# A new issue order for the five queues of a fused attention and state-space kernel

## The chip, the cores and the metric

The kernel runs on one core of a Trainium2 chip. The core has five instruction queues that matter here: TensorE (PE, matmuls, with its weight loads counted apart as PEld), VectorE (DVE), ScalarE (ACT), SyncE (SP) and GpSimd (POOL). Each executes its own list of instructions in the order in which the list is written, and the queues wait for one another by semaphores. SP, ACT and POOL also issue DMA transfers, which then run beside the engines. The metric is the device time of one execution in microseconds. Three executions are shown, and their median is the kernel's time.

## The reference

Two independent parts are computed from bfloat16 inputs, and their outputs are put side by side into one array of 1 x 2048 x 1280.

```python
def _A_ref(x, wqkv, wo):              # S = 2048, D = 640, 32 heads of 20
    qkv = (x @ wqkv).reshape(B, S, 3, H, Dh).transpose(2, 0, 3, 1, 4)
    q, k, v = qkv[0], qkv[1], qkv[2]
    off = arange(8) * 2               # each position sees itself and 7 before it, in steps of 2
    logits = einsum("bhsd,bhswd->bhsw", q, kg) * Dh ** -0.5
    attn = softmax(where(mask, logits, -1e9))
    o = einsum("bhsw,bhswd->bhsd", attn, vg)
    return o.transpose(0, 2, 1, 3).reshape(B, S, D) @ wo

def _B_ref(u, A_re, A_im, B_re, B_im, C_re, C_im, log_dt, Dskip):   # L = 2048, D = 640, N = 192
    dt = exp(log_dt)[:, None]
    P = exp((dt * (A_re + 1j * A_im))[:, :, None] * arange(L))
    K = einsum("dn,dnl,dn->dl", C, P, dt * B).real
    y = irfft(rfft(u padded to 2L) * rfft(K padded to 2L))[:L]
    return y + u * Dskip
```

## The kernel before

The state-space part works on five chunks of 128 channels (NCH = 5). It starts with a preparation (`partB_prep`). `load` (L127 to L132) brings the parameters in, each in four quarters u = 0 to 3 of 32 partitions. Of `B_A_re`, ACT's queue loads the quarters 0 and 2, and SP's the quarters 1 and 3 (L131). `decays` (L168) turns `B_A_re` times dt into columns: PE multiplies a quarter with a diagonal matrix DG (L156 on DVE; L163 and L166 on PE, into `ps_tr`), and ACT copies each quarter from `ps_tr` into `alpha`, a part of the tile LPB (L173). `fill` (L175) is DVE's work on `B_A_im`: dt·A_im/2π is reduced and split into three bfloat16 pieces, hi (L186), mid (L188) and lo (L189), once for the first chunk (128x192: `hi_188`, `mid_189`, `lo_190`) and once for the four others (128x768: `hi_367`, `mid_368`, `lo_369`). Transfers of SP and POOL (L194) move the pieces into the tile LPA; one transfer carries the pieces of both planes of a quarter. `weights` (L221 to L228, the tiles p10, p11, p20, p21 and CN) and `coefficients` (L237, the tile cT) prepare B times C. SP also loads U (four transfers of 640 KB, L914), the constants T2 (1 MB, L907), EA and BD, and Dskip (Dn).

For each chunk, `exps_chunk` fills the table R with ACT's Exp (L256) from LPB's `alpha`, which every instruction reads over all four quarters. `phase_table` fills the tables TA and TX with ACT's Sin (L311) from PE's products of LPA (`ps_ph`, L303 and L307). Exp and Sin use different tables of ACT, so each change costs an ACT_TABLE_LOAD. DVE multiplies R with TA and TX into PG, Q and X (L332) and PG with k's power into Y (L366); PE sums X·Y over the states into the convolution kernel (L380, L385). Then come the Fourier stages: PE and ACT (L399 to L408), DVE's products (L432), the inverse on PE and ACT (L445, L446), a transfer of half a spectrum by SP (L415, P2 and Zdram), and u·Dskip (UD, DVE's L460, moved to `UDdram` by POOL, L461).

The attention part starts in the last chunk: projections of k (L553), q (L571) and v (L584), a halo of k (`k_halo`, L562), products and logits (L604, L615), softmax, the weighted sum of v (DVE's L690 and PE's L697 into `ps_o`) and the output projection (L732 on). The inverse transform of the state-space part ends between them (L787).

What sets the order is a table. The program is written as one long function (`body`), which records instructions in a natural order. At its end `pin` (L866) goes through the five strings of `ORDER` (L808), one for PE, DVE, ACT, SP and POOL in turn. A string lists runs "start+count" in hexadecimal, counted in the engine's own instructions as recorded, and `pin` chains each instruction to the one before it in that list. This is a dependence without a semaphore: it only fixes the queue's order. Waits for data between the engines come from the tiles as before. A second table, `PLACES`, sets which bank of PSUM a product uses.

Of the kernel before, what the change touches and what calls it, by code (L numbers as in the profile page):

```python
# [744 lines left out]
class Inverse:  # L745
# [63 lines left out]
    '3+3 0+3 6+6 54+c c+8 1c+8 38+4 40+4 78+c 2c+8 60+c 14+8 24+8 6c+c 84+c 48+4 50+4 34+4 3c+4 90+c 44+4 4c+4 a8+c 9c+c b4+8 c4+8 bc+8 cc+8 e0+4 e8+4 '  # L809
    '35c+c 374+c d4+8 380+c dc+4 e4+4 9a4+c fc+80 ec+4 f4+4 f0+4 f8+4 2fc+10 17c+80 32c+10 31c+10 9b0+c 30c+10 1fc+c0 344+8 354+8 2bc+40 34c+8 33c+8 368+c '  # L810
    '394+8 3a4+8 3b4+4 3bc+4 3d4+80 3c8+4 3d0+4 3b8+4 3c0+4 38c+8 39c+8 3c4+4 3cc+4 454+40 3ac+8 4e4+10 494+40 504+10 9bc+c 4f4+10 4d4+10 534+80 524+8 '
    '51c+8 514+8 5b4+80 52c+8 654+10 634+20 664+10 704+80 694+8 6a4+8 9c8+c 68c+8 674+8 784+40 6b4+c 6c4+4 67c+8 7c4+40 684+8 6c0+4 6c8+8 6d4+4 69c+8 6ac+8 '
    '6d0+4 6d8+c 6ec+8 6e4+8 6f4+10 814+80 914+10 804+10 924+10 894+40 934+20 8d4+40 954+20 9f4+80 974+10 a74+40 984+8 ab4+40 99c+8 98c+8 af4+80 ec8+c '
    '994+8 9d8+4 9e0+4 b74+40 9d4+4 9dc+4 bb4+40 9e8+4 9f0+4 9e4+4 9ec+4 c24+10 c04+10 ed4+c bf4+10 c54+8 c64+8 c14+10 c9c+40 c34+10 c5c+8 c6c+8 c44+8 '
    'cdc+40 c80+4 c88+4 c4c+8 ee0+c c7c+4 c84+4 c8c+4 c94+4 c74+8 d1c+40 c90+4 c98+4 d6c+40 e2c+20 d5c+10 dac+40 e4c+20 dec+40 e8c+10 e7c+10 e6c+10 f34+40 '
    'ea4+10 f74+40 ebc+c e9c+8 eb4+8 fb4+40 eec+8 efc+8 ff4+40 ef4+8 f04+14 f1c+4 1034+40 f24+4 f2c+4 f18+4 f20+4 1074+40 f28+4 f30+4 10d4+10 10b4+20 '
    '1388+c 10e4+10 111c+8 112c+8 1394+c 10fc+8 10f4+8 114c+4 1154+4 115c+40 1104+10 13a0+c 1150+4 1158+4 1114+8 1124+8 1134+8 119c+40 113c+4 1144+4 1140+4 '
    '1148+4 11dc+50 12fc+10 12ec+10 134c+10 130c+20 122c+40 132c+20 126c+80 1364+10 135c+8 137c+c 13f4+40 1374+8 1434+40 13ac+8 13bc+8 1474+40 13d4+4 '
    '13dc+4 13b4+8 13c4+8 14b4+40 13d8+4 13e0+4 14f4+40 13cc+8 1588+8 1598+8 13e8+4 13f0+4 13e4+4 13ec+4 1590+8 15a0+8 1534+40 15a8+8 1574+14 15b4+4 15bc+4 '
    '15d0+4a 15b0+4 15b8+4 16a4+10 161a+40 169a+a 16b4+10 17ce+19 15c0+4 15c8+4 16d4+10 16c4+10 165a+40 1704+a 15c4+4 15cc+4 170e+80 16fc+8 16e4+8 178e+40 '  # L820
    '17e7+a 16ec+8 18b1+a 16f4+8 17f1+80 18bb+a 18d9+4a 18c5+a 1871+40 18cf+a 1923+40 19f9+10 19cb+a 1963+68 19e9+10 1a27+10 1a09+a 1a37+10 1a6b+10 19d5+14 '
    '1a5b+10 1a7b+10 1a13+14 1a8b+10 1af7+a 1a9b+10 1a47+14 1b01+a 1ab3+8 1acf+28 1aab+8 1abb+14 1b0b+a 1b1d+a 1b51+a 1b37+a 1b27+10 1b6b+a 1b41+10 1b5b+10 '
    '1b15+8 1b85+14 1b75+10 1bc1+50 1c4d+28 1c39+14 1c11+28 1c75+14 1b99+28 1cb5+3c 1cb1+4 1c89+28 1cf1+14 1d2d+3c 1da1+4 1d05+28 1dc5+8 1d69+28 1dcd+28 '
    '1d91+10 1da5+20 1e15+4 1df5+10 1e1d+4 1e05+10 1e21+10 1e51+8 1e31+10 1e19+4 1e7d+2 1e41+10 1e59+4 1ea1+c 1e9f+2 1ecd+2 1ee3+2 1e5d+10 1ef5+4 1ecf+4 '
    '1e6d+10 1e7f+20 1ead+20 1ed3+10 1ee5+10 1ef9+8 1f11+4 1f4f+a 1f2a+5 1f01+10 1f15+15 1f2f+20 1f5e+5 1f59+5 1f6f+10 1f63+4 1f7f+30 1fb9+4 1f67+8 1faf+a '
    '1fbd+4 2001+5 1fc1+20 2015+8 2006+5 1fe1+10 2061+5 1ff1+10 200b+a 201d+4 2066+5 2021+40 2075+c 206b+a 2081+20 20c1+a 20a1+10 20d5+4 20b1+10 20dd+20 '
    '20d9+4 20fd+8 2109+10 2105+4 2119+10 20cb+a 2129+1a 2173+a 2143+30 217d+20 21c7+a 21a7+20 21a2+5 219d+5 21db+a 21d6+5 21d1+5',
    '0+1 3+1 5+1 4+1 8+1 a+1 2+1 9+1 7+1 6+1 b+1 10+1 1f+1 21+1 e+1 1e+1 20+1 11+1 22+1 12+2 16+1 d+1 23+1 17+1 14+1 24+1 18+1 15+1 27+1 19+2 c+1 1b+2 28+1 '
    '2f+2 34+1 33+1 1d+1 35+1 31+1 36+1 25+1 32+1 29+1 37+2 26+1 39+1 2a+2 3b+1 f+1 2c+2 3a+1 2e+1 3c+1 3e+3 3d+1 41+1 44+1 48+1 42+1 45+1 43+1 47+1 46+1 '
    '4b+1 49+2 4c+2 50+1 5e+1 4f+1 4e+1 51+2 57+1 62+1 54+1 53+1 58+1 55+2 5b+1 5a+1 59+1 5d+1 5c+1 70+1 60+1 5f+1 61+1 63+1 65+3 64+1 6a+1 1+1 76+1 68+1 '  # L830
    '6d+1 84+1 6e+1 69+1 6b+1 88+1 74+1 6c+1 9d+1 6f+1 73+1 75+1 ad+1 79+1 71+2 77+2 7a+1 7d+1 b1+1 7b+2 81+1 7e+3 86+1 82+2 87+1 85+1 89+1 8b+2 8a+1 8d+2 '
    '96+1 95+1 90+1 8f+1 9b+1 91+1 93+1 92+1 9c+1 97+1 94+1 9a+1 99+1 98+1 9e+4 a4+2 a2+1 a6+1 a3+1 a7+1 aa+1 a8+1 ab+2 c6+1 ae+1 a9+1 af+2 b2+1 b4+2 b3+1 '
# [345 lines left out]
```

## Time and profile before

| | us |
|---|---|
| median of three runs | 390.82 |
| lowest, highest run | 389.01, 391.63 |
| the profiled execution's span | 389.9 |
| PE busy (8677 matmuls) | 338.0 |
| DVE busy | 356.1 |
| ACT busy | 311.8 |
| PE, longest waits for its own instructions on the chain | 2.16, 2.06, 2.00, 1.95 |

The profile is one execution. A line of a timeline has the start, the length, the engine, the line of the kernel, the operation, the tile written and the tile read, the number of instructions it puts together, and in brackets the idle time before it and what ended that. "SPq" and "ACTq" are the issuing of transfers by these queues. A line of a stretch has its start and end, its length, the busy time of PE, PEld, DVE, ACT and POOL (with the count of instructions), the granted PE clock as a share of full speed, the DMA engines' busy share, and GB/s. A line of the waits has who waited for whom: in total, how often, and the longest.

### The profile page before, as it was taken

What the parts mean: (1) busy time and instruction counts of PE and PEld (TensorE: products, weight loads), DVE (VectorE), ACT (ScalarE), POOL (GpSimd) and SP (SyncE); (2) the same over time, 40 slices, a digit from 0 to 9 for tenths busy, and PEclk for the clock granted to TensorE, in tenths of its full rate; (3) what the DMA queues carried; (4) which work ended last, traced back from release to release, by engine and by line L of the source; (5) the groups of instructions that cost most, each with busy time, mean ns of one, the idle gap of its engine ahead of it and who ended that gap; (6) DMA issues with size and microseconds to landing.
All of it is one profiled execution on the core that took longest, in us unless ns stands there. A gap on an engine that the chain in (4) does not pass through costs nothing.

```text
span 389.9 us, 18862 instructions
## 1 busy us (share of the span) xinstructions
PE 338.0 (87%) x8677; PEld 250.9 (64%) x8677; DVE 356.1 (91%) x353; ACT 311.8 (80%) x524; POOL 49.9 (13%) x102
## 2 busy tenths in 40 slices
PE   1286989788898899988888999999999997789993
PEld 0275878677787778877777576556656775344561
DVE  8989899997999999999999998999988996897971
ACT  3999999799999999999998766455987746576761
POOL 8545001021000000100000100000030100011220
PEclk9998899699999999999999999999999999788998
DMA  6499304035021410151049662110773589399254
GB/s 161 109 192 208 121 13 163 6 103 121 29 84 34 109 32 31 57 131 40 2 118 152 144 133 71 34 30 2 166 248 100 163 192 204 70 254 282 81 141 110
DMA packets 39471, 43.30 MB, mean 111 GB/s; under 512 B 24768, under 2 KB 33952, under 8 KB 38752
## 3 DMA queue, kind: packets, MB, share of 16 engines
q1 hardware_dynamic: 34384, 29.34, 32.4%
q0 software_dynamic: 4112, 12.22, 11.5%
q8 instruction: 68, 1.11, 1.3%
q10 hardware_dynamic: 896, 0.54, 0.5%
q14 instruction: 11, 0.09, 0.1%
HBM read 19.63 MB, written 14.16 MB: 87 GB/s over the span
## 4 chain that ended last, share of the span: by engine, by line
PE 44%; ACT 25%; DVE 18%; issue 6%; DMA 4%; SPq 2%; POOL 0%; ACTq 0%; DVEq 0%; POOLq 0%
ACT R L256 7%; PE ps_k L553 6%; PE ps_q L571 6%; PE ps_v L584 6%; DVE Y L366 5%; ACT A L408 4%; DVE X L332 4%; PE ps_o L697 3%; ACT A L403 3%; PE ps_k L380 3%; PE ps_k L385 3%; PE ps_op L732 3%; PE ps_l L615 2%; PE ps_ia L445 2%; PE ps_f L399 2%
## 5 line engine op out<-in xcount | busy, mean ns | idle before, releaser
L366 DVE TENSOR_TENSOR Y<-PG 128x3072 bf16<-128x3072 bf16 x60 | 102.9, 1750 | 3.0 <-PE ps_k L385 2.8
L256 ACT ACTIVATE R<-LPB 128x192 bf16<-128x192 f32 (+1 forms) x169 | 57.7, 420 | 0.1
L380 PE MATMUL ps_k<-Y,X 128*32 128x64 bf16 x2176 | 46.9, 240 | 7.0 <-issue 2.7
L385 PE MATMUL ps_k<-Y,X 64*32 64x64 bf16 x2176 | 45.5, 234 | 0.7 <-issue 0.6
L380 PEld LDWEIGHTS <-X 128*32 128x32 bf16 x2176 | 34.8, 117 | 15.4 <-issue 6.8
L408 ACT CAST A<-ps_f 128x1024 bf16<-128x1024 f32 x40 | 40.4, 1038 | 3.5 <-PE ps_f L407 3.4
L385 PEld LDWEIGHTS <-X 64*32 64x32 bf16 x2176 | 32.8, 113 | 8.8 <-issue 1.1
L332 DVE TENSOR_TENSOR X<-R,TX 128x1536 bf16<-128x1536 bf16 x40 | 37.3, 950 | 0.3 <-PE ps_k L385 0.3
L311 ACT ACTIVATE TX<-ps_ph 128x768 bf16<-128x768 int16 x40 | 32.2, 838 | 3.7 <-PE ps_ph L307 3.7
L690 DVE TENSOR_TENSOR prod<-v,atp 128x1536 bf16<-128x1536 bf16 (+3 forms) x32 | 31.6, 1022 | 3.7 <-PE ps_o L697 3.7
L303 PE MATMUL ps_ph<-LPB,LPA 128*64 128x256 bf16 x288 | 29.3, 308 | 4.0 <-ACT A L408 1.3
L311 ACT ACTIVATE TA<-ps_ph 128x768 bf16<-128x768 int16 x30 | 24.3, 843 | 1.8 <-PE ps_ph L307 1.7
L407 PE MATMUL ps_f<-A,T 128*128 128x128 bf16 x320 | 22.3, 217 | 3.3 <-ACT A L408 1.3
L604 DVE TENSOR_TENSOR prod<-qT,kT 128x1024 bf16<-128x1024 bf16 (+1 forms) x16 | 22.9, 1486 | 1.2 <-ACT qT L572 0.8
L584 PE MATMUL ps_v<-xT,wv 128*32 128x512 bf16 x400 | 23.2, 379 | 0.0
L553 PE MATMUL ps_k<-xT,wkq 128*128 128x512 bf16 x100 | 23.1, 380 | 0.0
L407 PEld LDWEIGHTS <-T 128*128 128x128 bf16 x320 | 19.1, 96 | 6.1 <-issue 3.3
L571 PE MATMUL ps_q<-xT,wkq 128*128 128x512 bf16 x100 | 22.6, 379 | 0.0
L446 ACT CAST Z<-ps_ia 128x1024 bf16<-128x1024 f32 x20 | 19.6, 1014 | 3.4 <-PE ps_ia L445 2.2
L401 ACT ACTIVATE A<-ps_f,sign 128x1024 bf16<-128x1024 f32 x20 | 21.5, 1149 | 0.2 <-PE ps_f L399 0.2
L332 DVE TENSOR_TENSOR PG<-R,TA 128x768 bf16<-128x768 bf16 (+1 forms) x30 | 19.8, 685 | 1.8 <-ACT TA L311 1.3
L399 PE MATMUL ps_f<-BD,U 128*64 128x128 bf16 x320 | 21.0, 285 | 0.1
(157 smaller groups left out, 696.1 us busy)
## 6 DMA issues: line engine op xcount, KB each, us to landing
P<-A SPq DMA_DIRECT2D x16, 256.0 KB, 3.1
Zdram<-Z SPq DMA_DIRECT2D x16, 256.0 KB, 3.7
Z<-Zdram SPq DMA_DIRECT2D x8, 512.0 KB, 7.0
U<-in_B_u_dram SPq DMA_DIRECT2D x4, 640.0 KB, 9.5
UDdram<-UD POOLq DMA_DIRECT2D x10, 256.0 KB, 2.7
Z<-UDdram POOLq DMA_DIRECT2D x4, 640.0 KB, 6.7
out_dram<-ysb SPq DMA_DIRECT2D x32, 80.0 KB, 3.9
out_dram<-ob POOLq DMA_DIRECT2D x8, 160.0 KB, 3.4
```

The source lines that it names most:

```text
L256: exp = lambda o, i, m: nc.scalar.activation(out=o, in_=i, func=ACT.Exp, scale=m)
L311: last = nc.scalar.activation(out=dst, in_=words.rearrange("p b (q e f) -> p b q (e f)", e=8, f=4), func=ACT.Sin, scale=PI_LO / 32768.0)
L332: TT = lambda o, a, b, op: V.tensor_tensor(out=o, in0=a, in1=b, op=op)
L366: nc.vector.tensor_tensor(out=Y[:].rearrange("p q (b a) f -> p q b a f", a=8), in0=fa, in1=gb, op=A.mult)
L380: MM(ps[32 * g:32 * g + 32, t], lhsT=X[:, q, x, :, f], rhs=Ys[k][:, q, :, f], start=(t == 0 and n == 0), stop=False, tile_position=(0, 32 ...
L385: MM(ps[32 * g:32 * g + 32, t], lhsT=X[hb, q, x, :, f], rhs=Ys[k][hb, q, :, f], start=False, stop=(n == len(sets) - 1), tile_position=(64 ...
L407: last = MM(ps[:, kk], lhsT=C["T2"][:, 8 * b + kk, :], rhs=A1[:, :, 8 * b + kk, :], start=(kk % 4 == 0), stop=True, skip_group_check=True)
L408: nc.scalar.copy(out=A1[:, :, 8 * b:8 * b + 8, :], in_=ps[:].rearrange("p k (j g) -> p j k g", g=4))
L553: MM(ps[:, i], lhsT=self.wk[:, kt, 128 * ct:128 * ct + 128], rhs=self.x4[:, kt, 2 * i:2 * i + 2, 256 * hf:256 * hf + 256], start=(kt == 0) ...
L571: MM(ps[:, i], lhsT=self.wq[:, kt, 128 * ct:128 * ct + 128], rhs=self.x4[:, kt, 2 * i:2 * i + 2, 256 * hf:256 * hf + 256], start=(kt == 0) ...
L584: MM(ps[32 * sc:32 * sc + 32, i], lhsT=self.wv[:, kt, d + i::DH], rhs=self.xT[:, kt, 512 * sc:512 * sc + 512], start=(kt == 0), stop=(kt = ...
L690: nc.vector.tensor_tensor(out=p2.rearrange("p (d i) -> p d i", i=ni), in0=self.v2[:, 4 * j0:4 * j0 + 4 * nj, off:off + ni], in1=at[:, w, i ...
```

## The change

Only the five strings of `ORDER` differ. `PLACES`, the tiles, the instructions and their operands are the same; the file grows by nine lines, so that every line below the table has a number higher by nine (L914 becomes L923). The beginning of SP's string, before and after:

```diff
-    '2+1 1+1 0+1 3+1 19+1 c+1 7+1 4+1 14+1 6+1 d+1 a+1 9+1 8+1 17+1 1a+1 b+1 e+2 5+1 11+1 10+1 15+1 13+1 12+1 1e+2 18+1 20+1 23+2 1b+2 22+1 21+1 1d+1 16+1 '
...
+    '0+3 a+1 6+1 d+1 9+1 c+1 7+1 5+1 b+1 8+1 24+1 1a+1 17+1 f+1 16+1 1e+1 13+1 1c+1 11+2 15+1 e+1 10+1 19+1 3+1 21+2 4+1 23+1 18+1 1f+1 1b+1 14+1 1d+1 20+1 '
...
```

SP's queue at its start. The two loads of `B_A_re` (the quarters 1 and 3) stand in its rows 3 and 7 before. The first eight transfers before:

```order
L123 DMA ldt_105<-in_B_log_dt_dram 32x20 x2
L1140 DMA ident_58<-ident_c 128x128
L132 DMA B_A_re_112<-in_B_A_re_dram 32x5x192
L909 DMA Dn_223<-in_B_Dskip_dram 32x160
L132 DMA B_C_re_138<-in_B_C_re_dram 32x5x192
L140 DMA mix_124<-c_mix 128x288
L132 DMA B_A_re_112<-in_B_A_re_dram 32x5x192
L905 DMA BD_75<-c_BD 128x512
```

The same queue now, its rows 16 to 27:

```order
L194 DMA LPA_101<-lo_190 32x2x192
L194 DMA LPA_101<-mid_368 32x2x576
L194 DMA LPA_101<-hi_188 32x2x192
L194 DMA LPA_101<-mid_189 32x2x192
L915 DMA EA_77<-c_EA 128x256
L194 DMA LPA_101<-hi_188 32x2x192
L194 DMA LPA_101<-lo_190 32x2x192
L918 DMA Dn_223<-in_B_Dskip_dram 32x160
L132 DMA B_A_re_112<-in_B_A_re_dram 32x5x192
L194 DMA LPA_101<-mid_368 32x2x576
L194 DMA LPA_101<-lo_369 32x2x576
L132 DMA B_A_re_112<-in_B_A_re_dram 32x5x192
```

The two loads now stand in rows 24 and 27. Ahead of these rows, from row 3, come the other parameters and constants, then U (row 11), Dn, mid_189 (row 13), T2 (row 14) and U again (row 15).

DVE's queue at the end of the preparation, with the second plane's mid_368 and lo_369. Before:

```order
L187 TENSOR_TENSOR m1_388<-tg32_381,hi_367 128x768
L188 CAST mid_368<-m1_388 128x768
L221 TENSOR_TENSOR p11_554<-B_B_re_128,B_C_im_143 128x768
L189 TENSOR_TENSOR lo_369<-m1_388,mid_368 128x768
L223 TENSOR_TENSOR p11_554<-p11_554,p21_555 128x768
L226 TENSOR_SCALAR CN_125<-p11_554,dts_154 128x192 x4
L332 TENSOR_TENSOR PG_577<-R_231,TA_279 128x1536
```

And now:

```order
L189 TENSOR_TENSOR lo_369<-m1_388,mid_368 128x768
L221 TENSOR_TENSOR p10_545<-B_B_re_128,B_C_re_138 128x768
L221 TENSOR_TENSOR p10_421<-B_B_re_128,B_C_re_138 128x192
L223 TENSOR_TENSOR p10_545<-p10_545,p20_546 128x768
L223 TENSOR_TENSOR p10_421<-p10_421,p20_422 128x192
L221 TENSOR_TENSOR p11_427<-B_B_re_128,B_C_im_143 128x192
L222 TENSOR_TENSOR p21_555<-B_B_im_133,B_C_re_138 128x768
L223 TENSOR_TENSOR p11_554<-p11_554,p21_555 128x768
L226 TENSOR_SCALAR CN_125<-p11_554,dts_154 128x192 x4
L223 TENSOR_TENSOR p11_427<-p11_427,p21_428 128x192
L226 TENSOR_SCALAR CN_125<-p10_421,dts_154 128x192
L226 TENSOR_SCALAR CN_125<-p11_427,dts_154 128x192
```

The pieces are finished earlier in DVE's list, and the weights, those of the first chunk included, stand behind them. PG (L332) follows in both.

ACT's queue around its first table of exponentials, R. Before, its rows 6 to 15:

```order
L132 DMA B_A_re_112<-in_B_A_re_dram 32x5x192
L173 COPY LPB_102<-ps_tr_168 128x48
L173 COPY LPB_102<-ps_tr_173 128x48
L173 COPY LPB_102<-ps_tr_178 128x48
L173 COPY LPB_102<-ps_tr_183 128x48
L256 ACTIVATE R_231<-LPB_102 128x48x4 x42
L237 CAST cT_167<-ps_tr_433 128x4x48
L256 ACTIVATE R_231<-LPB_102 128x48x4 x3
L311 ACT_TABLE_LOAD
L311 ACTIVATE TA_279<-ps_ph_280 128x2x384
```

And now, the rows 8 to 19:

```order
L173 COPY LPB_102<-ps_tr_178 128x48
L173 COPY LPB_102<-ps_tr_183 128x48
L256 ACTIVATE R_231<-LPB_102 128x48x4 x23
L237 CAST cT_167<-ps_tr_433 128x4x48
L256 ACTIVATE R_231<-LPB_102 128x48x4 x6
L237 CAST cT_167<-ps_tr_447 128x4x48
L256 ACTIVATE R_231<-LPB_102 128x48x4 x2
L237 CAST cT_167<-ps_tr_475 128x4x48
L256 ACTIVATE R_231<-LPB_102 128x48x4 x7
L237 CAST cT_167<-ps_tr_461 128x4x48
L256 ACTIVATE R_231<-LPB_102 128x48x4 x7
L173 COPY LPB_102<-ps_tr_489 128x4x48
```

The copies of cT, which use DVE's CN by way of PE, now lie among R's exponentials. Then follow the table load and the first TX, ahead of the two TA. Over the rest of the program runs of instructions change places in the same manner on all five engines. Among them, the last transposes of x on SP and `k_halo` on PE stand later, DVE's UD steps (L460) too, and the outputs on SP are spread differently.

115 rows, old and new, of the table ORDER are left out of this document.

## The prediction

> **What bounds the kernel now.** I read the page's busy times first, then the chain of waits, then a table of stretches. The busy lines say that no engine is full from end to end; the chain's shares say that TensorE, ScalarE (ACT) and VectorE (DVE) each carry a part of the end; only the stretches say where.
>
> ```profile
> span 389.9 us, 18862 instructions
> PE 338.0 (87%) x8677; PEld 250.9 (64%) x8677; DVE 356.1 (91%) x353; ACT 311.8 (80%) x524; POOL 49.9 (13%) x102
> PE 44%; ACT 25%; DVE 18%; issue 6%; DMA 4%; SPq 2%; POOL 0%; ACTq 0%; DVEq 0%; POOLq 0%
> 0.00:8.56 8.56, 1.29 (x12) 0.90 (x12) 6.81 (x21) 2.29 (x7) 7.40 (x19) 1.00 0.61 151
> 8.56:33.02 24.46, 15.10 (x220) 12.98 (x221) 23.17 (x48) 22.75 (x68) 12.87 (x24) 1.00 0.93 164
> 33.02:128.75 95.73, 83.04 (x2803) 71.23 (x2801) 89.93 (x80) 93.56 (x169) 11.14 (x22) 0.93 0.29 82
> 128.75:213.76 85.01, 75.94 (x2392) 65.72 (x2386) 84.68 (x72) 82.50 (x130) 2.81 (x6) 1.00 0.31 75
> 213.76:329.00 115.24, 114.18 (x2220) 74.33 (x2217) 108.57 (x89) 77.28 (x90) 7.49 (x19) 1.00 0.51 122
> ```
>
> In the last five lines stand the stretch, its length, then the busy time of PE, its weight load, DVE, ACT and POOL. From 8.56 to 128.75 ACT is the full engine (22.75 of 24.46, then 93.56 of 95.73). DVE takes over until 213.76 (84.68 of 85.01), and PE until 329 (114.18 of 115.24). So a late start of ACT is carried from one full engine to the next, and only their small idle remains can absorb it. What releases ACT at 8.56 is the place to look at, in ACT's and SP's timelines:
>
> ```profile
> 8.33 0.20 ACT L173 COPY LPB<-ps_tr 128x48 f32<-128x48 f32 x1 [0.91 <-PE ps_tr L166]
> 8.56 3.65 ACT L256 ACTIVATE R<-LPB 128x192 bf16<-128x192 f32 x14
> 2.13 0.72 SPq L132 DMA_DIRECT2D B_A_re<-in_B_A_re_dram  x1
> 4.94 0.57 SPq L132 DMA_DIRECT2D B_A_re<-in_B_A_re_dram  x1
> DMA to landing us min/median/max: 2.6/2.8/3.0
> ```
>
> The exponentials R (L256) need the decay table LPB. It is written by four copies (L173), one for each quarter of B_A_re, behind PE transposes (L163, L166). Two quarters are loaded by SP, at 2.13 and 4.94; a transfer lands 2.6 to 3.0 us behind its issue. So the last lands by 7.9, and R begins at 8.56, some 0.7 later.
>
> **The change, part by part.** No instruction is added, removed or resized, so the busy times stay; only places in five queues differ.
>
> *SP's two loads.* They go from rows 3 and 7 of SP's queue to rows 24 and 27, behind seven transfers that carry DVE's pieces (mid, lo, hi) and behind U twice, T2 and EA. In the profile such a transfer holds its queue while its data are missing, and SP also stands after large ones:
>
> ```profile
> SPq L194 <- DVE m L187: 1.9, 2, 1.6
> 17.18 0.59 SPq L194 DMA_DIRECT2D LPA<-mid  x1
> 17.82 2.11 SPq L914 DMA_DIRECT2D U<-in_B_u_dram  x2
> 19.97 3.32 SPq L909 DMA_DIRECT2D Dn<-in_B_Dskip_dram  x1
> 24.04 4.97 SPq L914 DMA_DIRECT2D U<-in_B_u_dram  x2
> 29.05 4.48 SPq L194 DMA_DIRECT2D LPA<-hi  x1
> ```
>
> The first line is SP waiting at L194 for DVE, in total 1.9 us in 2 waits: the queue does not pass over a transfer that isn't ready. The last load now stands behind lo_369, the last piece that DVE makes. When is lo_369 made? DVE works almost without a gap through this preparation in the profile:
>
> ```profile
> 4.09:27.97 23.88, 23.50 (x63) 1.00 0.85 167
> 24.18 0.95 DVE L221 TENSOR_TENSOR p<-B_B_re,B_C_im 128x768 f32<-128x768 bf16 x1
> 25.05 0.95 DVE L189 TENSOR_TENSOR lo<-m,mid 128x768 bf16<-128x768 f32 x1
> 25.92 0.95 DVE L223 TENSOR_TENSOR p<-p,p 128x768 f32<-128x768 f32 x1
> 26.90 1.07 DVE L226 TENSOR_SCALAR CN<-p,dts 128x192 bf16<-128x192 f32 x4
> L221 DVE TENSOR_TENSOR p<-B_B_re,B_C_re 128x192 f32<-128x192 bf16 x1 | 0.3, 350 | 0.0
> ```
>
> (The first line is the stretch 4.09 to 27.97 with DVE's busy time alone: 0.4 idle.) The same steps in another order, with no more idle, still end at 27.97, ahead of L332. Behind lo_369 the new order has four steps of 128x768, four of 128x192 and six CN (L226). A 128x768 step takes 0.87 from its start to the next (24.18 to 25.05); a 128x192 one, 0.35 less the same overlap of 0.08, 0.27; a CN 1.07/4, with its share of the step, 0.25 as an estimate. That is 3.48 + 1.08 + 1.5 = 6.06, so lo_369 is ready at 27.97 − 6.06 = 21.9, and mid_368, one step ahead, at 21.0. mid_368's first transfer is SP's row 17 and the last load row 27: eleven issues. An issue is 0.58 to 0.61, with 0.04 between two (17.18 to 17.82 is 0.64). Ten steps put the last issue's start at 21.0 + 6.4 = 27.4. lo_369 is long ready then, so mid_368 sets the pace. The load lands 2.8 later, at 30.2, and R begins 0.7 behind that: 30.9, if SP never stands.
>
> Upper end: SP stands behind U and T2 as long as it stood in the rows above, 3.32 at Dn less a plain 0.6, and 4.48 less 0.6: 2.7 + 3.9 = 6.6, so R at 37.7. I take R at 32.2, nearer the lower end: one U and T2 are in flight when the loads' turn comes (the other U is issued ahead of DVE's first piece), where the rows had U in pairs. ACT's start moves by 32.2 − 8.56 = **+23.6** (bounds +22.3 and +29.1). Nothing hides it: ACT runs its list in order, and behind the four copies stand 23 instructions of R; nothing that could run sooner is ahead of them.
>
> *DVE's loss.* Its first step on R (PG) starts at 29.12 in the profile, when R's 45 instructions and a table are done:
>
> ```profile
> 29.12 0.96 DVE L332 TENSOR_TENSOR PG<-R,TA 128x1536 bf16<-128x1536 bf16 x1 [1.16 <-ACT TA L311]
> L256 ACT ACTIVATE R<-LPB 128x192 bf16<-128x192 f32 x45 | 11.6, 348 | 0.0
> 20.28 1.28 ACT L311 ACT_TABLE_LOAD   x1
> 28.18 0.84 ACT L311 ACTIVATE TA<-ps_ph 128x768 bf16<-128x768 int16 x1
> ```
>
> In the new order ACT has R's 45, five small copies (0.3 each), the table load, a TX and two TA ahead of it: 32.2 + 11.6 + 1.5 + 1.3 + 3 × 0.75 = 48.9. So DVE stands from 28 to 49, and loses 19.8, a little less than ACT.
>
> *What comes back.* Of ACT's 23.6, ACT's own idle may absorb 24.46 − 22.75 = 1.7 up to 33.02, since the tables' waits there end while R is still running: I take all of it. Of the 95.73 − 93.56 = 2.2 up to 128.75 I take half, 1.1, since those waits are on work that shifts too. Also, ahead of the chunk's table with which the chain leaves ACT at 128.75, the new order has 2.7 us less of ACT's work: that is the difference of two sums, over all of ACT's instructions ahead of that table in the one order and in the other, each with its own duration in the profile. Part of it may be missed later; I take 2.0.
>
> *Instruction packets and the tail.* The order is laid out for packets that arrive late. In the profile:
>
> ```profile
> q8 instruction: 68, 1.11, 1.3%
> 68.27 2.16 issue
> PE ps_o L697 <- issue: 5.7, 3, 2.0
> 353.40:389.90 36.50, 29.57 (x626) 16.92 (x622) 24.17 (x27) 20.02 (x39) 6.26 (x12) 0.96 0.52 145
> ```
>
> Three waits of PE for its own instructions in the tail cost 5.7 together, one at 68.27 costs 2.16. If the order takes all from the path it gains 7.9; if none, 0. The packets are as many as before and PE does not run earlier, so their places in time cannot all be avoided; I take −2, near the lower end. [...]
>
> *Other moves.*
>
> ```profile
> DVE UD L460 <- DMA UDdram<-UD: 2.3, 2, 1.9
> ```
>
> k_halo and the last x transposes on PE go later, UD's steps on DVE too, and outputs on SP earlier. In the stretch to 213.76 DVE has 0.3 us idle and in that to 329 PE 1.1, so none can gain more than 1.4 there. What they might lose is a wait like the 1.9 us of the line above, the longest that DVE's UD step stood for its transfer. I take 0, with −1.4 and +1.9 in the range.
>
> Sum, against the profiled execution: 389.9 + 23.6 − 1.7 − 1.1 − 2.0 − 2.0 = 406.7. The median of the runs, 390.82, is 0.9 above that execution, so the forecast is 406.7 + 0.9, about **408 us**, or 4.3% slower.
>
> **The rivals.**
>
> *A. The loads are not held (the other side: faster or the same).* If SP passed over transfers whose data are missing, or if the last load landed by 9 us, R would start as before. Then the packets alone count: 390.8 − 2, at most − 7.9, so 383 to 391, about 388. It decides from the landing: each us beyond 8 is a us for ACT. Against it stands the row of SP waiting at L194 for DVE, and that ten issues ahead of it take 6.4 us even without waits. In its favour is only that no row shows a B_A_re load standing behind a waiting transfer.
>
> *B. DVE's idle and the reordering absorb more.* DVE is idle 95.73 − 89.93 = 5.8 from 33.02 to 128.75. If the new order fills it, so that DVE enters its own stretch with 5.8 us more done than shifted, and its loss is 19.8 and not 23.6, the end is, with half of the packets' 7.9, 390.8 + 19.8 − 5.8 − 4.0 = about 401. For it: DVE is the next to be full, so its account decides. Against it: its idle time there lies behind ACT's tables, which are late too.
>
> *C. SP stands behind U and T2.* R at 37.7 gives 408 + 5.5 = 413 to 414. For it: the 3.32 and 4.48 of the rows above. Against it: fewer large transfers at once.
>
> **How the numbers follow.** The likeliest case, R at 31 to 34 with the sum above, gets 0.52 and spans 403 to 411. B gets 0.22 (398 to 403), C 0.18 (411 to 418), A 0.05, and 0.03 is for all else. The range 398 to 417 takes in the first, B, and nearly all of C. About 1% (3.9 us) is what a measurement of this kernel can tell from no change. Faster by over 1% needs A with more than half of the packets: 0.03. Within 1% takes the rest of A and the outer edge of B: 0.05. Slower: 0.92.
>
> **What would show it.** In the new profile SP should show the two B_A_re loads issued at about 26 and 28, the four copies of L173 ending at 31 to 33, R's first at 32.2, ACT idle from about 5 to there, PG's first at about 49 and DVE idle 20 us ahead of it. The waits should name PE or its weight load at L163 waiting for B_A_re. The stretch behind R should be as long as before less about 7 us. If R begins before 10, the reading of SP's queue is wrong. If it begins at 32 and the time is under 400, the account of what ACT's and DVE's idle absorb is wrong. If PE shows as much waiting for issue as before, the packets' term is 0.

## The result and the profile after

The changed kernel takes 482.12 us, the median of four runs (480.23 to 483.13), where the kernel before stood at 390.4, the median of four. The ratio is 1.2355, with the interval 1.2312 to 1.2397: 92 us slower, not 18. Some executions of some kernels fall into a slower state (of the six of e22 below, one took 403.20 us and the others 395.86 to 398.83), and ratios and intervals leave these out, while the times beside them are medians of all. The profiled execution ran 480.23, with a span of 478.5.

The page of the kernel after, its span, busy times, instruction queue and three groups. A group has its line, engine, operation, output and inputs and count, then busy time and mean ns, and last the idle time just before it with what ended most of it:

```profile
span 478.5 us, 18861 instructions
PE 355.3 (74%) x8677; PEld 254.7 (53%) x8677; DVE 358.9 (75%) x353; ACT 315.1 (66%) x524; POOL 48.2 (10%) x102
q8 instruction: 68, 1.11, 1.0%
L366 DVE TENSOR_TENSOR Y<-PG 128x3072 bf16<-128x3072 bf16 x60 | 103.2, 1752 | 28.6 <-PE ps_k L385 28.4
L380 PE MATMUL ps_k<-Y,X 128*32 128x64 bf16 x2176 | 45.9, 241 | 23.1 <-DVE X L332 22.6
L584 PE MATMUL ps_v<-xT,wv 128*32 128x512 bf16 x400 | 25.1, 404 | 18.7 <-DMA wv<-in_A_wqkv_dram 18.7
```

The counts of PE, DVE and ACT are as before, and DVE's and ACT's busy times within 3.3 us; only PE is 17.3 us busier. So most of the time lost is idle time. The three groups say who stands: DVE's Y for PE, PE's L380 for DVE's X, and PE's v projection for a load. None of the three was a term of the prediction.

A table of stretches of the kernel after. The columns are start and end, length, busy time of PE, PEld, DVE, ACT and POOL, the granted PE clock, the DMA share and GB/s. The cuts lie within some 1.5 us of where the instructions now stand that stood at 8.56, 33.02 (this one roughly), 128.75, 213.76, 302.15 and 353.4 of before:

```profile
0.00:32.70 32.70, 1.00 (x13) 0.75 (x14) 26.48 (x64) 2.11 (x7) 19.26 (x44) 1.00 0.79 170
32.70:57.13 24.43, 15.39 (x216) 11.17 (x216) 5.95 (x7) 23.55 (x69) 3.11 (x7) 1.00 0.46 79
57.13:156.00 98.87, 88.52 (x2840) 73.34 (x2840) 87.91 (x77) 91.64 (x162) 7.14 (x13) 0.90 0.20 59
156.00:265.00 109.00, 80.56 (x2344) 67.64 (x2345) 86.31 (x72) 86.01 (x138) 3.24 (x6) 0.89 0.23 50
265.00:361.50 96.50, 86.69 (x1645) 55.47 (x1639) 81.58 (x71) 58.70 (x67) 3.72 (x12) 0.98 0.37 91
361.50:441.00 79.50, 53.80 (x1048) 29.55 (x1041) 46.43 (x39) 33.26 (x49) 4.28 (x7) 0.74 0.53 132
441.00:478.50 37.50, 29.32 (x617) 16.80 (x585) 24.27 (x28) 19.80 (x38) 7.40 (x14) 1.00 0.52 137
```

The first line is the late start, 24 us more than before. The fourth took 85.01 before, with DVE busy 84.68: now DVE does as many steps and stands 22.7 us beside them. The sixth has 53.80 of PE's work in 79.50. From 57 to 441 no engine is as full as the fullest was before. By those instructions themselves, the loss is about 24.1 to the start of R, 2.3 up to the TX that stood at 128.75 before, 25.4 to 213.76, 8.9 to 302.15, 26.4 to 353.4, and 1.5 behind it: 88.6 together, the difference of the two spans.

The head went as the prediction had it. SP's, ACT's and DVE's timelines of the kernel after (start, length, engine, line, operation, in brackets the idle time before and what ended it):

```profile
27.61 0.58 SPq L132 DMA_DIRECT2D B_A_re<-in_B_A_re_dram  x1
29.56 0.59 SPq L132 DMA_DIRECT2D B_A_re<-in_B_A_re_dram  x1
```

```profile
32.36 0.30 ACT L173 COPY LPB<-ps_tr 128x48 f32<-128x48 f32 x2 [1.06 <-PE ps_tr L166]
32.70 5.92 ACT L256 ACTIVATE R<-LPB 128x192 bf16<-128x192 f32 x23
```

```profile
48.16 0.56 DVE L332 TENSOR_TENSOR PG<-R,TA 128x768 bf16<-128x768 bf16 x1 [19.82 <-ACT TA L311]
```

The loads are issued at 27.61 and 29.56 (forecast 26 and 28), R starts at 32.70 (32.2), and DVE's first PG at 48.16 (48.9), 19.0 us later than before (19.8). The pace was another, though. SP's row behind T2 and U takes 2.82 instead of some 0.6:

```profile
19.87 2.82 SPq L194 DMA_DIRECT2D LPA<-lo  x1
```

So the transfer of mid_368 is issued at 22.79, where DVE had made that piece by 21.2: it was this stand of SP, and not mid_368, that set the time. What follows R was not foreseen. The waits of the kernel after, who waited for whom: total, how often, longest:

```profile
PE ps_tr L163 <- DMA B_A_re<-in_B_A_re_dram: 31.4, 3, 22.6
DVE Y L366 <- PE ps_k L385: 28.4, 13, 6.0
ACT v L586 <- PE ps_v L584: 27.8, 7, 21.6
DVE PG L332 <- ACT TA L311: 25.3, 5, 19.8
PE ps_k L380 <- DVE X L332: 22.6, 9, 8.6
PE ps_v L584 <- DMA wv<-in_A_wqkv_dram: 18.7, 1, 18.7
...
PE ps_k L385 <- issue: 2.2, 2, 1.3
PE ps_o L697 <- issue: 1.5, 1, 1.5
PE ps_ph L303 <- issue: 0.8, 1, 0.8
PE ps_k L380 <- issue: 0.2, 1, 0.2
```

Two single places can be followed by hand. **First, wv.** POOL's timeline of the kernel after:

```profile
347.73 0.12 POOL L621 MEMSET ql<- 32x8 bf16 x1
...
369.62 0.56 POOL L773 DMA_DIRECT2D Z<-UDdram  x1 [21.76 <-DMA Z4dram<-Z]
370.17 0.91 POOL L532 DMA_DIRECT2D wv<-in_A_wqkv_dram  x1
```

and of the kernel before:

```profile
286.93 0.86 POOL L532 DMA_DIRECT2D wv<-in_A_wqkv_dram  x1
...
308.68 0.56 POOL L773 DMA_DIRECT2D Z<-UDdram  x1 [18.64 <-PE ps_l L615]
```

The load of wv has no input that the kernel computes; before it stood ahead of the transfer Z, which waits long for its data in either order. Now it stands behind it, is issued at 370.17, and PE begins its v projection at 382.1, after 18.7 us of waiting. **Second, a late X.** DVE's timeline of the kernel after:

```profile
241.82 1.75 DVE L366 TENSOR_TENSOR Y<-PG 128x3072 bf16<-128x3072 bf16 x1
243.49 0.95 DVE L332 TENSOR_TENSOR X<-X 128x1536 bf16<-128x1536 bf16 x1
250.43 3.43 DVE L366 TENSOR_TENSOR Y<-PG 128x3072 bf16<-128x3072 bf16 x2 [5.99 <-PE ps_k L385]
```

and PE's beside it:

```profile
244.50 0.67 PE L380 MATMUL ps_k<-Y,X 128*32 128x64 bf16 x32 [8.56 <-DVE X L332]
```

The X at 243.49 is a piece of one half of a chunk, and stands in DVE's list behind the first Y of the next half. PE's sum that needs it stands early in PE's list, so PE waits 8.56 us for a step of 0.95; then DVE finds no free Y, because PE frees them late, and waits 5.99. The two engines stand in turn. Before, the same step of X ran at 181.03, ahead of the next half; now it stands behind that half's first Y.

### The profile page after: what moved, and what is told of

It reads as the page before. It is cut to its first block, busy times and chain, and to the rows that moved or that the text cites. A ratio compares the mean times of both kernels' runs of the same rounds, so it can differ in the third digit from the quotient of the medians.

```text
span 478.5 us, 18861 instructions
## 1 busy us (share of the span) xinstructions
PE 355.3 (74%) x8677; PEld 254.7 (53%) x8677; DVE 358.9 (75%) x353; ACT 315.1 (66%) x524; POOL 48.2 (10%) x102
## 5 line engine op out<-in xcount | busy, mean ns | idle before, releaser
L366 DVE TENSOR_TENSOR Y<-PG 128x3072 bf16<-128x3072 bf16 x60 | 103.2, 1752 | 28.6 <-PE ps_k L385 28.4
L380 PE MATMUL ps_k<-Y,X 128*32 128x64 bf16 x2176 | 45.9, 241 | 23.1 <-DVE X L332 22.6
L256 ACT ACTIVATE R<-LPB 128x192 bf16<-128x192 f32 (+1 forms) x169 | 59.1, 417 | 0.1
L380 PEld LDWEIGHTS <-X 128*32 128x32 bf16 x2176 | 33.9, 118 | 31.0 <-DVE X L332 24.4
L385 PE MATMUL ps_k<-Y,X 64*32 64x64 bf16 x2176 | 45.0, 235 | 2.2 <-issue 2.2
L332 DVE TENSOR_TENSOR X<-R,TX 128x1536 bf16<-128x1536 bf16 x40 | 36.9, 951 | 4.0 <-PE ps_k L385 3.4
L332 DVE TENSOR_TENSOR PG<-R,TA 128x768 bf16<-128x768 bf16 (+1 forms) x30 | 19.9, 687 | 25.9 <-ACT TA L311 25.3
L584 PE MATMUL ps_v<-xT,wv 128*32 128x512 bf16 x400 | 25.1, 404 | 18.7 <-DMA wv<-in_A_wqkv_dram 18.7
L385 PEld LDWEIGHTS <-X 64*32 64x32 bf16 x2176 | 32.8, 113 | 10.8 <-issue 5.0
L303 PE MATMUL ps_ph<-LPB,LPA 128*64 128x256 bf16 x288 | 29.2, 315 | 3.6 <-ACT TA L311 1.8
L584 PEld LDWEIGHTS <-wv 128*32 128x32 bf16 x400 | 14.8, 141 | 26.2 <-DMA wv<-in_A_wqkv_dram 19.0
L586 ACT CAST v<-ps_v 128x1024 bf16<-128x1024 f32 x10 | 10.0, 1012 | 27.8 <-PE ps_v L584 27.8
L407 PE MATMUL ps_f<-A,T 128*128 128x128 bf16 x320 | 25.3, 232 | 1.9 <-ACT A L403 1.1
L163 PE MATMUL ps_tr<-DG,B_A_re 32*128 32x32 bf16 x20 | 2.2, 192 | 32.2 <-DMA B_A_re<-in_B_A_re_dram 31.4
L571 PE MATMUL ps_q<-xT,wkq 128*128 128x512 bf16 x100 | 22.6, 379 | 1.7 <-DMA wkq<-in_A_wqkv_dram 1.7
```

The source lines that it names most:

```text
L256: exp = lambda o, i, m: nc.scalar.activation(out=o, in_=i, func=ACT.Exp, scale=m)
L303: MM(o[64 * hh:64 * hh + 64, :, 0:8], lhsT=L[:, 64 * hh:64 * hh + 64], rhs=rhs, start=first, stop=last, skip_group_check=True, tile_positi ...
L332: TT = lambda o, a, b, op: V.tensor_tensor(out=o, in0=a, in1=b, op=op)
L366: nc.vector.tensor_tensor(out=Y[:].rearrange("p q (b a) f -> p q b a f", a=8), in0=fa, in1=gb, op=A.mult)
L380: MM(ps[32 * g:32 * g + 32, t], lhsT=X[:, q, x, :, f], rhs=Ys[k][:, q, :, f], start=(t == 0 and n == 0), stop=False, tile_position=(0, 32 ...
L385: MM(ps[32 * g:32 * g + 32, t], lhsT=X[hb, q, x, :, f], rhs=Ys[k][hb, q, :, f], start=False, stop=(n == len(sets) - 1), tile_position=(64 ...
```

## The experiments

Prices below are (ratio − 1) × 390; the intervals are some ±2 us wide, up to ±3.7. By this the whole change costs 92. "B" is the order before, "A" the one after, and "from 33" means from the instructions that stood at 33 us of before. Edits of single rows are shown as rows of the queue, those of many as the strings taken. Four theories meet in the expectations: at first, that the late start and a few single misplaced moves each have a price, and that these add up; against it, that the late start is half recovered behind, or that the moves hide one another; later, that what remained lay in DVE's order alone, and, against that, that the orders of PE and ACT do not fit DVE's either.

**The head.** e1 gives the loads back their early places in A; e2 does the one move alone in B, putting both loads behind SP's fourth U.

SP's queue in e1, against A:

```diff
+L132 DMA B_A_re<-in_B_A_re_dram 32x5x192
 L132 DMA B_B_re<-in_B_B_re_dram 32x5x192
 L137 DMA LPB<-c_F 128x1056
 L132 DMA B_C_re<-in_B_C_re_dram 32x5x192
+L132 DMA B_A_re<-in_B_A_re_dram 32x5x192
...
-L132 DMA B_A_re<-in_B_A_re_dram 32x5x192
 L194 DMA LPA<-mid 32x2x576
 L194 DMA LPA<-lo 32x2x576
-L132 DMA B_A_re<-in_B_A_re_dram 32x5x192
```

> The kernel after, with SP's two loads of B_A_re put back to the fourth and eighth place of SP's queue. Theory 1 (the lost time lies in many places of the new order, each with its own price): the first R begins near 8.6, as in the profile before. But DVE's weights of the first chunk (CN) are only made at 28 in the new order, and ACT's fifth copy (cT, L237) stands behind 23 of R, so ACT stops at about 14.5 and goes on at about 28.8; R ends at about 35 instead of 45, and of the 24 us of the head only about 10 come back: 472 us. Theory 2 (the rest of the loss is only what follows from the late start: engines out of step): with the start back the rest goes too, about 395 to 415 us.

474.04 us, ratio 1.2176 (1.2122 to 1.2229): 7 us come back of 24. ACT's timeline of e1 shows why:

```profile
9.87 5.93 ACT L256 ACTIVATE R<-LPB 128x192 bf16<-128x192 f32 x23
...
30.06 0.32 ACT L237 CAST cT<-ps_tr 128x192 bf16<-128x192 f32 x1 [14.26 <-PE ps_tr L166]
```

R begins at 9.87, but behind 23 exponentials ACT stands 14.26 us at the copy cT, which needs the first chunk's CN from DVE; and DVE now makes that after lo. The late start has two locks, and e1 opened one.

SP's queue in e2, against B:

```diff
-L132 DMA B_A_re<-in_B_A_re_dram 32x5x192
...
-L132 DMA B_A_re<-in_B_A_re_dram 32x5x192
...
 L914 DMA U<-in_B_u_dram 32x64x160 x2
+L132 DMA B_A_re<-in_B_A_re_dram 32x5x192 x2
```

> The kernel before, with only the two loads of B_A_re moved on SP, behind the fourth U (issue at about 29.1 and 29.7, landing at 32.5). Theory 1 (a late start is carried to the end, less what ACT's idle absorbs): R begins at 33.2, 24.6 later; less 1.7 and 1.1, the time is 412 us. Rival (DVE's 5.8 us of idle and the rest absorb more): about 404 us. Theory 2 (a late start sets off waits in all later stages): 450 us or more.

419.38 us, ratio 1.0804 (1.0748 to 1.0859): +31. Here R starts at 39.28, 30.7 later than before (ACT's timeline of e2):

```profile
39.28 10.72 ACT L256 ACTIVATE R<-LPB 128x192 bf16<-128x192 f32 x42
```

All of the delay reaches the end, within the 2 us of the interval: an absorption of 2.8 would have given 27.9, and the interval is 29.2 to 33.5.

**The head and the rest apart.** e5 keeps B to the instructions at 128.75 and takes A behind; e7 takes A to 48 and B behind.

```diff
-all five queues: A
+e5: B up to the instructions at 128.75, then A
+e7: A up to the instructions at 48, then B
```

> All five queues in the order of before up to what starts by 128.75 us in its profile, and in the new order behind that. Theory 1 (the loss lies in the places of the new order themselves): in the profile after, about 26 of the 91 us are lost by that point, so 65 us are left: 454 us. Theory 2 (the late start sets off the rest): the start is not late, so 390 to 400 us.

452.63 us, ratio 1.1581 (1.1525 to 1.1636): +62.

> All five queues in the new order up to what starts by 48 us in the profile after (its first PG), and in the order of before behind that. Theory 1: only the late start is left, carried to the end one for one as in the run with the late loads: 390 + 24 = 414 us. Theory 2 (late start sets off the rest): 450 us or more.

416.05 us, ratio 1.0684 (1.0624 to 1.0744): +27. Together they make 89 of the 92. In e7 the same DVE steps run 24 to 27 us later than before from 40 us of before to the end (table below).

**wv.** e3 moves one row of POOL in A:

```diff
 L621 MEMSET ql 32x8
+L532 DMA wv<-in_A_wqkv_dram 128x5x640
 L773 DMA Z<-UDdram 32x4x2560
-L532 DMA wv<-in_A_wqkv_dram 128x5x640
```

> The kernel after, with the load of wv (L532) moved on POOL's queue by one place, ahead of the first load of Z from UDdram (L773). Theory 1: wv is issued at about 348 instead of 370, PE's wait of 18.7 us for it goes, and nearly all of it reaches the end: 464 us. Rival (DVE and ACT are late there anyway, or the load of Z is late next): 475 us or more.

461.94 us, ratio 1.1884 (1.1844 to 1.1925): 18 us come back (20 by the medians). POOL's timeline of e3:

```profile
350.78 0.92 POOL L532 DMA_DIRECT2D wv<-in_A_wqkv_dram  x1
...
372.69 0.57 POOL L773 DMA_DIRECT2D Z<-UDdram  x1 [21.00 <-DMA Z4dram<-Z]
```

wv is issued 19.4 us earlier, and Z waits as before. PE's wait for wv is gone from the list.

**X.** e4 moves DVE's steps of X in A so that the pieces of one X stand together, without a Y between them:

```diff
-L332 TENSOR_TENSOR X<-R,TX 128x12x128
-L366 TENSOR_TENSOR Y<-PG 128x3072
-L332 TENSOR_TENSOR X<-R,TX 128x12x128 x3
-L366 TENSOR_TENSOR Y<-PG 128x3072 x5
+L332 TENSOR_TENSOR X<-R,TX 128x12x128 x2
+L366 TENSOR_TENSOR Y<-PG 128x3072
+L332 TENSOR_TENSOR X<-R,TX 128x12x128 x2
+L366 TENSOR_TENSOR Y<-PG 128x3072 x5
...
```

> The kernel after, with DVE's later pieces of each X (L332) moved up to stand right behind its first piece. Theory 1: PE's waits at L380 for X (22.6 us in 9 waits) and DVE's waits for PE behind them (28.4 us at Y in 13 waits) shrink by most of their size, and 15 to 20 us reach the end: 462 to 467 us. Rival (another wait takes their place, since DVE is the full engine of these stages and only trades one late step for another): 475 us or more.

464.76 us, ratio 1.196 (1.1904 to 1.2016): 15 us come back (17 by the medians). The waits of e4:

```profile
DVE Y L366 <- PE ps_k L385: 13.5, 12, 3.0
...
PE ps_k L380 <- DVE X L332: 3.6, 2, 1.8
```

PE's waits for X fall from 22.6 to 3.6, and DVE's for PE from 28.4 to 13.5.

e22 turns it around: in B a single X step of 0.87 us is put some 20 us later, behind the next half's first Y (DVE's queue):

```diff
-L332 TENSOR_TENSOR X<-X 128x12x128
...
-L366 TENSOR_TENSOR Y<-PG 128x3072 x3
+L366 TENSOR_TENSOR Y<-PG 128x3072
+L332 TENSOR_TENSOR X<-X 128x12x128
+L366 TENSOR_TENSOR Y<-PG 128x3072 x2
```

> The kernel before, with one single step of DVE moved: the last piece of X for the second unit of one half (X_5272, 0.87 us) stands behind the first Y of the next half, as in the new order, 20 us later. Theory 1: PE's queue stands at L380 for it while DVE goes on, then DVE stands at the second Y for PE, so 6 to 9 us are lost: 396 to 400 us. Rival (DVE is full there, and only changes the order of its work): under 393 us.

398.13 us, ratio 1.0186 (1.0148 to 1.0223): +7. The waits of e22:

```profile
PE ps_k L380 <- DVE X L332: 9.4, 1, 9.4
...
DVE Y L366 <- PE ps_k L385: 10.1, 5, 4.6
```

One misplaced step, one wait of 9.4 on PE, and from it several on DVE.

**What is left when the three known causes are mended.** e8 has B's head to 33, A behind, wv first and X together:

```diff
-all five queues: A
+all five queues: B up to the instructions at 33, then A
+POOL: wv ahead of Z
+DVE: the pieces of each X together
```

> The order of before up to 33 us (the start), the new order behind that, with wv ahead of Z on POOL and each X's pieces together on DVE. Theory 1 (the prices add up): 482 - 24 - 17 - 20 = 421 us, with what is left in the stretches of 130 to 160 and 200 to 280 us of before and in the tail. Rival (the mended waits hide others, which come up when all three are gone): 430 us or more.

420.86 us, ratio 1.0801 (1.0754 to 1.0848): the three prices add up as expected, and +31 remain.

**Where the remainder lies.** The tail first: e6 has B to the instructions at 300 and A behind on all five queues; e18 the same on DVE alone.

```diff
-all five queues: B
+e6: B up to the instructions at 300, then A
+e18: B, and DVE alone as in e6
```

> The kernel before, with all five queues in the new order from what starts at 300 us on (wv is loaded by then, so its wait is not in it). Theory 1 (the prices add up): the tail's 10 us, 400 us. Rival (the tail's loss follows from the late wv and the lower clock in the profile after): 388 to 392 us, or less if fewer waits for instructions reach the end.

398.83 us, ratio 1.024 (1.0197 to 1.0283): +9.

> The kernel before, with DVE's queue in the new order from what starts at 300 us on. In the run with DVE's queue alone in the new order the shift fell by 3 us over this stretch. Theory 1 (the tail's loss of 10 us in the profile after comes from other queues): 387 to 390 us. Rival: 395 us or more.

390.23 us, ratio 1.0028 (0.9994 to 1.0062): no difference that can be told. So the tail costs 9, and DVE's part of it nothing. PE's waits for its own instructions are not the tail's price: e6 shows, in its waits,

```profile
PE ps_o L697 <- issue: 3.9, 2, 2.9
```

where before had 5.7. A rival for these 9 us is left open: the lower granted clock. In e6 it is at half from 337.4 to 354.5, 17 us, where before has half for 10 us from 336 to 353, and PE is 4.2 us busier in all (342.2 against 338.0). Over the span it is 0.952 to 0.970 in e6's six runs and 0.961 to 0.996 in the seventeen runs of before beside them. The same stretch of e8, set against that of before (its line first; the granted clock follows POOL's time):

```profile
300.00:353.40 53.40, 47.59 (x1030) 29.02 (x1028) 46.47 (x41) 32.85 (x47) 3.94 (x7) 0.90 0.73 174
321.00:382.00 61.00, 56.20 (x1092) 30.56 (x1090) 48.41 (x42) 35.64 (x52) 3.41 (x6) 0.80 0.65 159
```

PE is almost full there in both, and takes 8.6 us more for some 60 more matmuls.

Then the middle, 130 to 290 us. e12 puts A's whole DVE list into B; e17 puts DVE's half steps in e8 back to their old inner order:

```diff
-DVE: B
+e12: DVE: A, the other four B
...
-e8's DVE list
+e17: e8's DVE list, each half's steps in B's inner order
```

> The kernel before with only DVE's queue in the new order. Theory 1 (DVE's order is the largest of the parts behind the start): the CN of the first chunk come 12 us later, so that ACT stands before its first cT until about 28.5, some 8 us, and PE waits at L380 for X as in the profile after, 15 to 20 us: 413 to 418 us. Rival (the waits come from how the five orders fit together, and DVE's alone against the old order of the others is as bad as all or worse): 430 us or more. Rival (it is the order of PE and ACT that makes the waits): under 405 us.

440.86 us, ratio 1.1297 (1.1257 to 1.1337): +51, far over the 413 to 418; the rival held.

> As the run with three places mended (421 us), but on DVE the steps of each half of a chunk (PG, Q, X, Y; L332 and L366) stand among themselves in the order of before, in the places that the new order gives to that half (in one half only X is so placed). Theory 1 (what is left between 130 and 280 us of before is also DVE making late what PE needs first, as the second unit's X and Y ahead of the first's): 15 of the 31 us go, about 406 us, the tail's 8 to 10 are left. Rival (it is the order of PE, ACT or UD's steps): 415 us or more.

430.2 us, ratio 1.0997 (1.0939 to 1.1054): +39, 8 more than e8 instead of 15 less. DVE's old inner order, which costs nothing beside B's PE, is worse beside A's PE than A's own. The time lies in the rival's range: a queue's order has no price by itself.

Four kernels then split the queues, all from 33 on:

```diff
-PE, ACT, DVE: B
+f1: PE and ACT: A; DVE: B
+f2: DVE: A; PE and ACT: B
+f3: f2 with the pieces of each X together
+f4: PE, ACT and DVE: A
```

SP and POOL are B's in all four.

> The kernel before, with PE's and ACT's queues in the new order from what starts at 33 us on, and DVE's, SP's and POOL's as before. Theory 3 (DVE's order makes the waits behind the start, PE and ACT only wait for it): no more than the tail's 9 us, 390 to 399 us. Theory 4 (what costs is how the orders fit together, and any half of the new order against a half of the old one loses as much as the whole): 410 us or more.

423.94 us, ratio 1.0881 (1.0841 to 1.092): +34. The theory that only DVE's order mattered (399 or less) falls.

> The kernel before, with DVE's queue in the new order from 33 us on and all others as before. It is the run with DVE's queue alone without the start's 10 us: 430 us by both theories. Theory 3 sees in it nearly all of the loss behind the start without wv (482 - 24 - 20 = 438, less 9 for the tail: 429).

431.58 us, ratio 1.1115 (1.1043 to 1.1187): +43. The waits of f2 have PE standing for X as in the kernel after:

```profile
PE ps_k L380 <- DVE X L332: 26.6, 9, 9.6
```

> As f2, but each X's pieces stand together on DVE. Theory 3: X's price is the same 17 us as in the kernel after, 413 us. Theory 4 (the fit): not the same, less than 10 or more than 25 us.

414.7 us, ratio 1.0632 (1.0587 to 1.0677): +25. Putting X together gives 19 back here, beside B's PE, and 15 in e4, beside A's: this one price is nearly the same in both, against theory 4.

> The kernel before, with PE's, ACT's and DVE's queues in the new order from 33 us on, and SP and POOL as before, so that neither the start nor wv is late. Both theories: 482 - 24 - 20 = 438 us, if SP's and POOL's order cost nothing else; below 430 they do.

434.66 us, ratio 1.1147 (1.1096 to 1.1198): +45, where 34 and 43 add up to 77. 434.66 is 3 us under the 438 expected if SP's and POOL's orders cost nothing but the late start and wv; so they cost nothing else that shows. That each side alone misses the other's old order, and both together only what doesn't fit in the new one, is a reading of these three and not shown.

The last two test one suspect in PE's order. Each Y is used by 32 matmuls of L380 and 32 of L385. In B the second half follows the first at once, for all 60 Y; in A other work, up to 94 matmuls, lies between them for 28 of the 60, which may keep Y from DVE. (The orders have another six: of the eight Y that serve two X, six are parted in seven places.) f5 is f1, and f6 is e8, with L385 right behind L380 for the 28; the seven places stay parted, by up to 30 matmuls (PE's queue):

```diff
 L380 MATMUL ps_k<-Y,X 32x64
+L385 LDWEIGHTS X
+L385 MATMUL ps_k<-Y,X 32x64
...
```

> As f1 (PE and ACT in the new order, 424 us), but on PE the second half of each sum over X and Y (L385) stands right behind its first half (L380). In the order of before the two halves of a Y are never parted; in the new one they are for 28 of the 60 Y, by up to 94 matmuls, so that a Y's place comes free for DVE only when PE has done, or waited for, what stands between. Theory 5 (this is what PE's order costs DVE): DVE's 17.6 us of waits at Y for PE shrink by half or more, and 8 to 15 us come back, 409 to 416 us. Rival (what stands between had to be done anyway, and other waits take over): 420 us or more.

419.2 us, ratio 1.0752 (1.0658 to 1.0846): 5 back of f1's 34, outside the expected 409 to 416. The intervals of the two runs leave anything from 1 to 9.

> As e8 (start, wv and X mended, 421 us), but with the two halves of each sum together on PE as in f5. Theory 5: DVE's 10.9 us of waits at Y for PE shrink by half or more, and 5 to 10 us come back, 411 to 416 us. Rival (DVE's new order was made for the parted sums): 418 us or more.

423.35 us, ratio 1.0895 (1.082 to 1.097): nothing back of e8's 31. DVE's waits for PE's L385 do fall (waits of f6),

```profile
DVE Y L366 <- PE ps_k L385: 8.3, 11, 2.7
```

from 10.9 in e8, but the time does not follow. These 28 parted sums are not what remains.

One rival for the remainder is seen in the profiles of all runs, and none separates it. In the eleven kernels with A's order of PE from 33 or 128.75 us on or throughout, PE is busy 352.8 to 358.9 us; in the nine with B's from 48 to 300, 336.6 to 345.2. The granted clock over the profiled spans is 0.895 to 0.935 in the eleven and 0.913 to 0.990 in the nine (0.913 and 0.928 in e12 and f2, the others at least 0.958). The number of matmuls is the same, and the late start, wv and X make little difference to it; e8, with these three mended, has

```profile
PE 354.0 (85%) x8677; PEld 255.2 (61%) x8677; DVE 360.3 (86%) x353; ACT 315.1 (75%) x524; POOL 48.9 (12%) x102
```

so up to 16 of its 31 us may be PE working longer at a lower granted clock (0.921 in e8, 0.966 before).

The shift of the same DVE steps against the kernel before, worked out from each pair of timelines (the median over the steps that lie in the 20 us from the given time of before on), shows where each price falls:

| at, us of before | after | e7 (A to 48) | e8 (mended) | f1 (PE, ACT) | e6 (tail) | e22 (one X) |
|---|---|---|---|---|---|---|
| 40 | 23 | 27 | −1 | 0 | 0 | 0 |
| 120 | 27 | 26 | 1 | 1 | 0 | 0 |
| 140 | 34 | 26 | 5 | 6 | 0 | 1 |
| 200 | 50 | 26 | 13 | 12 | 0 | 9 |
| 280 | 61 | 25 | 21 | 24 | 0 | 9 |
| 300 | 81 | 25 | 21 | 25 | 0 | 10 |
| 340 | 85 | 26 | 25 | 32 | 3 | 10 |
| 380 | 91 | 24 | 31 | 34 | 9 | 8 |

In the kernel after, the shift rises in steps: 23 at the start, from 27 to 61 between 120 and 280, 20 at once between 280 and 300 (wv), and 10 from there on. In e8 and f1 there is no such jump, but a rise of 16 to 18 us from 140 to 280 in smaller steps.

Swapping PE alone, ACT alone or POOL alone wasn't tried. None of the kernels is faster than the one before.

## Why the prediction was wrong

The direction was right, and so was the head, but the time lies far above the range. By the prediction's own steps:

- *SP's two loads, +23.6.* Right, as a place and as a size: SP does not pass over a transfer whose data are missing (in the kernel after it stood 4.3 us at L194 for DVE's mid), and R moved by 24.1. Rival A, that the loads are not held, falls. The pace was that of SP's stand of 2.82 at 19.87 and not of mid_368; the choice of 32.2, 1.3 above the time without any stand, took in most of that. (The upper end is 30.9 + 6.6 = 37.5, not 37.7.) What the step missed is that the loads are only one lock: with them early (e1), ACT waits for CN at 30.06.
- *DVE's loss, 19.8.* Right: the first PG starts 19.0 later, behind an idle time of 19.82. The steps between 40 and 60 us of before are already 23 late.
- *What comes back, −1.7, −1.1 and −2.0.* Wrong. The first two are 0 within what the runs tell: e2 carried 30.7 of delay to 31 at the end, and e7 its 25 (R at 33.74) to 27. That ACT's small idle remains take up no delay because what they wait for is delayed too is the likely reason; no run separates it. The 2.0 belongs to the new order behind the start, which neither run has; in the kernel after, the delay grew by 2.3 up to the TX that stood at 128.75, instead of shrinking. (ACT was not the full engine from the first, either: from 8.56 to 33.02 DVE has 23.17 of 24.46, ACT 22.75.) With that, rival B (401) falls. Rival C's mechanism, that SP stands behind large transfers, is seen in the kernel after (2.82 at 19.87) and more in e2 (4.91 at 28.21); as a price, 413 to 414, it falls too, since R starts at 32.70 and not at 37.
- *Instruction packets, −2.* Not settled, and small either way. PE's matmuls wait 4.7 us for instructions in the four rows above, where before had 9.6; but e2, which keeps the old order but for two loads, has 4.9 as well, so the fall isn't shown to come from the new order. The weight loads' waits for instructions rose from 49.5 to 60.7, summed over all their rows. "Issue" only says that the profile shows nothing else to wait for; that PE stands for instructions still to arrive is borne out by the trace of before for the four longest waits of matmuls (1.7 to 2.2 us), each of which ends 1.2 to 1.5 us behind the end of a packet of the instruction queue. In e6's tail the matmuls' wait at L697 fell from 5.7 to 3.9 while the time rose by 9. No run here separates what these waits are worth at the end.
- *Other moves, 0 with −1.4 and +1.9.* This is the step that failed. Behind R the prediction expected a stretch some 7 us shorter than before; it is 64.5 longer (445.8 against 381.3 by the two profiles). With the start in time (e5) the moves from 128.75 on cost 62, and 92 less the 24 of the start is 68: 18 to 20 for wv, 15 to 19 for DVE's late X, 9 in the tail, and some 20 in the middle, where the orders of PE and ACT and of DVE do not fit. These prices were each measured in another kernel, so their sum (62 to 68) is a check and not a proof that nothing is counted twice.

Why it failed can be said. The step bounded the loss by the longest wait that a row of the old profile showed at the places it named, 1.9 us. But the old profile shows the waits of the old order. A moved producer makes a wait that has no row yet: in e22 one step of X, moved by 20 us, made a wait of 9.4 on PE, where before its longest wait for X from 120 to 300 us was 1.5. Two of these could have been read beforehand. The order of POOL put wv behind Z, and the old timeline has Z standing 18.64 us for its data: the price was there, in a row. And DVE's order put X behind the next half's Y while PE's list kept the sum that reads it early. The step also reads DVE's 0.3 us and PE's 1.1 us of idle as a bound, "so none can gain more than 1.4 there". That bounds the gain alone. A full engine can still lose: DVE went from 84.68 of 85.01 to 86.31 of 109.00 in that stretch.

One small step mixes two measures: the 0.9 added at the end sets a median of times against a span, and the profiled execution of the kernel after has a time 1.7 above its span.

What stays open: which moves in the middle make up the 20. f1, f2 and f4 (+34, +43, +45) show that both sides take part and do not add up; f6 excludes the 28 parted sums. No single step of the rest was found, and how much of it is PE at a lower granted clock is not known.

## What to carry to other kernels

In this schedule, whose engines are full by turns, a delay at the start reached the end whole in both runs that made one alone (e2, e7): don't count idle remains against it unless a row shows them taking it up. For every instruction that a new order moves, look up its consumer's place in the other queue and what stands ahead of it in its own: a load without inputs behind a transfer that waits is as late as that transfer (20 us here), and one 0.87-us step put 20 us later cost 7 to 8. Orders of several queues are one plan, so a queue's list taken alone is no measure of that list: PE and ACT +34, DVE +43, all three +45.

## What the runs showed of the hardware

The load of B_A_re landed later amid other transfers. In e2 the two stand in the midst of U's transfers; SP's timeline and the span from issue to landing of L132's loads in e2:

```profile
28.21 4.91 SPq L132 DMA_DIRECT2D B_A_re<-in_B_A_re_dram  x2
...
DMA to landing us min/median/max: 2.6/3.5/9.2
```

The worst took 9.2 us, against 3.0 in the kernel before, and SP stood at the two for 4.91.

The granted PE clock was lower in two stretches of the kernel after: 0.89 from 156 to 265 and 0.74 from 361.5 to 441, where roughly the same work before ran at 1.00 and, from 300 to 353.4, at 0.90. PE was busy 355.3 us for the same 8677 matmuls, against 338.0. The clock is at half from 239.6 to 249.8 and from 365.9 to 386.4. These stretches begin within the waits of 8.6 and 18.7 on PE and end behind them, so that PE's first 5.3 and 4.2 us of work behind each wait run at half. The first 40 matmuls of the v projection (L584, 128x512) took 4.43 us there, from 382.14 on; the 40 from 386.95 on, at full clock, 2.33. But it is at half from 417.1 to 437.6 as well, with no wait of PE over 3.0 us there and PE busy 15.6 of the 20.5 us; what lowers it the runs do not show, nor how much of the 17.3 us lies on the path.
